# Two pairs' products with values in one TensorE step, short passes moved between VectorE and GpSimd, and unread products in TensorE's first planned waits

## The chip, the cores and the metric

The kernel runs on one core of one Trainium2 chip. Its time is device microseconds, the median over several executions. A profiled execution has a span (first to last recorded instruction) and a time of its own; both are given below. A core has five engines that run beside each other and wait on semaphores: TensorE (PE; its weight loads are PEld), VectorE (DVE), ScalarE (ACT), GpSimd (POOL), and SyncE (SP), which here issues all transfers, in order, from one queue.

## What is computed

Sliding-window attention with sink columns over 4 batches, 8 heads, 768 positions and a head size of 64, then a feed-forward layer over the 3072 x 512 result. The reference, cut:

```python
scores = scale * np.matmul(q, k.transpose(0, 1, 3, 2))
keep = (pos[None, :] < n_sink) | ((rel >= 0) & (rel < window))      # n_sink 4, window 128
a = softmax(np.where(keep, scores, -1e9))
x = heads_side_by_side(np.matmul(a, v))                             # 3072 x 512
h = np.maximum(x @ w_in, 0.0)                                       # 512 x 2048
out = (h * h) @ w_out                                               # 2048 x 512
```

## The kernel before

**Tiles.** The 3072 rows are eight chunks of 384 (half a batch each). In a chunk, heads go two by two: a *pair* has both heads on 128 partitions, and there are four pairs per chunk, 32 in all. Pairs 0 to 7 (the first two chunks) are *plain*: their scores are fp32 products on half the array each (L515). The other 24 have scores from operands split into a high and a low part, on the full array (L521).

**One pair's attention.** Per head and block of 128 queries: the scores go to one PSUM bank; VectorE scales, masks and takes the row maximum in one pass (L498); ScalarE takes the exponential and the row sum (L504). Then a small ScalarE pass (L593) and VectorE's reciprocal (L562) give the factor, and a scaling pass (L569 on GpSimd or VectorE, L567 on ScalarE) makes probabilities of it. The four sink columns go their own way. GpSimd copies them into a small buffer and subtracts the rounded part (`part_sinks`, L585 and L583, two short passes per head); for plain pairs TensorE transposes that buffer (L630), for the others VectorE does (L647) and four small transfers gather it (L653); a copy (L388) makes the operand `SK` of it. The window's probabilities are transposed too: for plain pairs on TensorE (L698, with copies out of PSUM by L388), for the others in 32 x 32 blocks on VectorE (L727, L731) into one array `T` for both heads, which four transfers put into DRAM (L744) and one gets back into `PT` (L757).

**Values.** `values` multiplies the transposed probabilities by the pair's values: for each head an fp32 product that takes half of the array's columns (L785; head 1 and head 0 beside each other), all into one PSUM bank, and then one full-array product for the sinks of both heads (L789, `VS` and `SK`). ScalarE copies the result as the high part of x (L801), VectorE subtracts it for the low part (L806).

**Feed-forward.** For each of 16 column blocks of the hidden layer (an *item*): twelve products with x (L837), a ReLU (L850) and a square (L854) on ScalarE, a product (L859) and a remainder (L866) on VectorE, then nine products with the second weights (L882). The weights come as packed 64-bit words; each of 32 rows costs VectorE four passes over 512 columns (L326, L333, L340, L350), the last of them sometimes on GpSimd, and ScalarE one (L346). The first chunks run as legs of 8, 16 and 8 items, the other six chunks as 16 items each.

**What sets the order.** All of this is handed to a `Plan`: `add(at, rank, emit, reads, writes, take, drop)` gives a step's engine or engines with a cost, a rank (its due time, counted in items), what it reads and writes, and the PSUM banks that it takes or frees. `order` then plays the engines forward by these costs and emits the steps in that order; on each engine the program runs in just that order. Banks: three for attention ("att"), two for the hidden layer, three for the output; the first chunk's attention may take any. A step marked "port" is one of VectorE's that GpSimd's steps keep clear of; with `SHARE` 0.5 an unmarked GpSimd step keeps clear of the first half of it. A switch of TensorE between full-array, half-row and half-column products is planned at 0.2.

## Time and profile before

| | us |
|---|---|
| median of three runs | 678.01 (lowest 676.47) |
| the profiled execution, its time | 677.97 |
| its span | 676.2 |
| TensorE busy / weight loads | 658.2 / 573.3 |
| VectorE busy | 445.5 |
| ScalarE busy | 392.5 |
| GpSimd busy | 125.2 |

In the profile, a row of the timeline has start, length, engine, line, operation, what it writes and reads, and how many instructions are merged; in brackets stand the idle time ahead of it and what ended that. In a list of stretches each engine has its busy time and its number of instructions, in the order PE, PEld, DVE, ACT, POOL, and then the granted TensorE clock, the share of the DMA engines and GB/s. A row of waits has the total, how often, and the longest. TensorE's matmuls are pipelined, and their ends are modelled: what one costs is best read from the start of one to the start of the next.

### The profile page before, as it was taken

To read this page: it belongs to the slowest core of one execution; us is meant where nothing else is said; L and a number is where in the kernel's file an instruction comes from. 1 tells how busy PE (TensorE), PEld (TensorE's weight loads), DVE (VectorE), ACT (ScalarE), POOL (GpSimd) and SP (SyncE) were. 2 spreads that over 40 slices of the span, in tenths; PEclk is the share of its full clock that TensorE was granted. 3 is DMA by queue.
4 is the path that set the end of the run, shared out by engine and by line. 5 is a ranking of instruction groups with operands and counts; after the bars stand their busy time and mean duration, and the time that the engine had idled before them with its cause. 6 is when DMAs were issued, how large, how long until landed. Compare 5 with 4: busy or idle time off the path is not lost.

```text
span 676.2 us, 11302 instructions
## 1 busy us (share of the span) xinstructions
PE 658.2 (97%) x3662; PEld 573.3 (85%) x3662; DVE 445.5 (66%) x1211; ACT 392.5 (58%) x1142; POOL 125.2 (19%) x319
## 2 busy tenths in 40 slices
PE   4999999999999999999999999999999999999996
PEld 3767889998888888898888888888889888899985
DVE  7899999878877656575667756665666664242221
ACT  5898644367665445566666676666677665542221
POOL 4542200033242221111112211111121221000000
PEclk9899999999999999999999999999999999999999
DMA  7856665025977544366555856557556853310001
GB/s 235 261 155 187 208 207 177 32 75 165 263 200 205 165 120 121 109 209 198 176 158 170 243 168 192 175 164 200 164 157 187 245 169 118 115 62 1 1 0 52
DMA packets 62547, 104.91 MB, mean 155 GB/s; under 512 B 10800, under 2 KB 39216, under 8 KB 62480
## 3 DMA queue, kind: packets, MB, share of 16 engines
q1 hardware_dynamic: 62480, 104.11, 51.8%
q8 instruction: 31, 0.51, 0.3%
q14 instruction: 36, 0.29, 0.1%
HBM read 78.72 MB, written 24.38 MB: 152 GB/s over the span
## 4 chain that ended last, share of the span: by engine, by line
PE 89%; DVE 7%; POOL 1%; issue 1%; DMA 1%; ACT 0%; SPq 0%; DVEq 0%; POOLq 0%
PE bank L882 39%; PE bank L837 38%; PE bank L785 5%; PE bank L521 5%; DVE P L498 2%; PE bank L789 1%; DVE w L350 1%; DVE f L333 1%; DVE f L340 1%; DVE f L326 1%; DVE P L569 1%; DMA kn<-in_k_dram 1%; POOL PSK_wide L585 1%; DVE gl L866 0%; PE bank L515 0%
## 5 line engine op out<-in xcount | busy, mean ns | idle before, releaser
L837 PE MATMUL bank<-x,w 128*128 128x384 f32 x1536 | 301.2, 338 | 0.0
L837 PEld LDWEIGHTS bank<-x,w 128*128 128x128 f32 x1536 | 266.1, 188 | 8.3 <-issue 1.4
L882 PE MATMUL bank<-w,gh 128*128 128x512 f32 x768 | 242.6, 397 | 0.0
L569 POOL TENSOR_SCALAR P<-P,small 128x260 f32<-128x260 f32 (+1 forms) x168 | 83.4, 513 | 415.6 <-DVE small L562 401.2
L882 PEld LDWEIGHTS bank<-w,gh 128*128 128x128 f32 x768 | 138.7, 188 | 22.4 <-issue 1.0
L882 PE MATMUL bank<-w,gl 128*128 128x512 f32 x384 | 151.8, 395 | 0.0
L850 ACT ACTIVATE r<-bank 128x384 f32<-128x384 f32 x128 | 62.7, 490 | 114.1 <-PE bank L837 112.8
L504 ACT ACTIVATE P<-P,nbs 128x260 f32<-128x260 f32 (+1 forms) x192 | 93.6, 488 | 60.3 <-DVE nbs L498 57.9
L859 DVE TENSOR_TENSOR bank<-bank,r 128x384 f32<-128x384 f32 x128 | 72.0, 563 | 77.4 <-ACT r L850 76.8
L498 DVE CUSTOM_DVE_ANT_0 P<-bank,maskA 128x260 f32<-128x260 f32 x128 | 53.1, 421 | 53.4 <-PE bank L521 52.8
L882 PEld LDWEIGHTS bank<-w,gl 128*128 128x128 f32 x384 | 72.1, 188 | 16.9
L866 DVE TENSOR_TENSOR gl<-bank,gh 128x384 fp32r<-128x384 f32 x128 | 71.1, 556 | 19.1 <-ACT gh L854 10.1
L854 ACT ACTIVATE gh<-r 128x384 fp32r<-128x384 f32 x128 | 66.7, 521 | 2.8 <-PE bank L882 0.7
L727 DVE STREAM_TRANSPOSE T<-P 128x384 f32<-128x384 f32 x96 | 45.3, 494 | 24.8 <-POOL P L569 24.7
L521 PEld LDWEIGHTS bank<-KS,QS 128*128 128x128 f32 x288 | 52.0, 188 | 5.7
L521 PE MATMUL bank<-KS,QS 128*128 128x260 f32 (+1 forms) x288 | 54.8, 277 | 0.0
L785 PE MATMUL bank<-PT,vn 128*64 128x256 f32 (+1 forms) x392 | 40.6, 347 | 0.0
L801 ACT CAST x<-bank 128x384 fp32r<-128x384 f32 x32 | 15.2, 474 | 42.1 <-PE bank L789 42.1
L785 PEld LDWEIGHTS bank<-PT,vn 128*64 128x64 f32 x392 | 25.7, 139 | 15.7 <-issue 6.3
L504 ACT ACTIVATION_READ_ACCUMULATOR P<-P,nbs 128x1 f32 x192 | 36.0, 188 | 0.0
L498 DVE CUSTOM_DVE_ANT_0 P<-bank,mask 128x128 f32<-128x128 f32 (+1 forms) x64 | 22.0, 353 | 19.3 <-PE bank L521 19.0
L374 ACT ACTIVATE sq<-sq,theta 128x256 bf16<-128x256 bf16 x64 | 32.2, 503 | 1.1
(99 smaller groups left out, 518.4 us busy)
## 6 DMA issues: line engine op xcount, KB each, us to landing
raw<-in_moe_w_dram SPq DMA_DIRECT2D x32, 512.0 KB, 4.0
half<-in_moe_w_dram SPq DMA_DIRECT2D x64, 256.0 KB, 3.9
via<-T SPq DMA_DIRECT2D x48, 192.0 KB, 3.1
PT<-via SPq DMA_DIRECT2D x12, 768.0 KB, 4.8
via<-T SPq DMA_DIRECT2D x48, 160.0 KB, 2.7
PT<-via SPq DMA_DIRECT2D x12, 640.0 KB, 5.4
kn<-in_k_dram SPq DMA_DIRECT2D x24, 264.0 KB, 3.9
qn<-in_q_dram SPq DMA_DIRECT2D x32, 192.0 KB, 3.7
```

Of the source, the lines that this page charges most:

```text
L498: nc.vector.tensor_tensor_reduce(Pt(h)[:, i, o : o + n], ps_[:, 0:n], mask[:, 0:n], -SCALE, BIG, ALU.add, ALU.min, nb)
L504: nc.scalar.activation(Pt(h)[:, i, o : o + n], Pt(h)[:, i, o : o + n], AF.Exp, bias=nb, scale=-1.0, accum_out=sm[:, h, i : i + 1],)
L521: nc.tensor.matmul(bank(key)[:, 0:n], QS(h)[:, cols], flat[:, a, c0 : c0 + n], start=(a == 0), stop=(a == 1),)
L569: {"POOL": nc.gpsimd, "DVE": nc.vector}[engine].tensor_scalar(a, a, rs[:, h, i : i + 1], 1.0, op0=ALU.mult, op1=ALU.mult)
L727: nc.vector.transpose(dst.rearrange("p c j b -> p j c b"), src.rearrange("p j (c b) -> p j c b", b=32))
L785: nc.tensor.matmul(xo[h * D : h * D + D, qs[0] * P : qs[0] * P + len(qs) * P], vn[:, kk, h, :], rhs(), start=(n == 0), stop=False, skip_gr ...
L837: nc.tensor.matmul(bank(key)[:, 0:TOK], wi[fc][:, i, cc * P : (cc + 1) * P], xt[:, cc, :], start=(cc == 0 and j == 0), stop=(cc == NCC - 1 ...
L850: lambda key=key, r=r: nc.scalar.activation(r(), bank(key)[:, 0:TOK], AF.Relu),
L854: ("ACT", 0.41), n - 9, lambda gh=gh, r=r: nc.scalar.activation(gh(), r(), AF.Square),
L859: lambda key=key, r=r: nc.vector.tensor_tensor(bank(key)[:, 0:TOK], bank(key)[:, 0:TOK], r(), op=ALU.mult),
L866: lambda key=key, gh=gh, gl=gl: nc.vector.tensor_tensor(gl(), bank(key)[:, 0:TOK], f32(gh()), op=ALU.subtract),
L882: nc.tensor.matmul(bank(okey), gt()[:, ts_], wo[f][:, i, :], start=(f == f0 and j == 0), stop=(f == f1 - 1 and j == 2),)
```

## The change

The edit has four parts and some that make room for them.

1. For pairs 8 to 31 the values of two pairs are one TensorE step: an even pair only leaves its functions in `waiting`; the odd pair's step runs both pairs' L785 products, into two banks, and then the first pair's sinks. The second pair's sinks are copied to `SK` after that and have a full-array step of their own. The step needs both pairs' transposed probabilities, so there are two arrays, `PT` and `PT2`, laid out by head. `T` holds one head instead of two; its four puts and the get are issued per head, the first head's with an earlier rank.
2. `part_sinks` may run on VectorE as well as on GpSimd, `SHARE` is 1.0 (an unmarked GpSimd step is planned behind the whole of a marked VectorE step), and the extra cost of a scaling pass on VectorE or ScalarE is 0.1 instead of 0.3.
3. Where the plan has TensorE wait more than 0.4 in the first 24 us for a step that takes a bank, `fill` writes products of the identity with itself into that bank; nothing reads them, and the step behind overwrites them.
4. The third chunk's attention has ranks that are six items earlier.

To make room: one array `G0` for the ReLU instead of two, one small `PSK` instead of two, the identity matrix lives in the scratch array `sq`.

```diff
-SHARE = 0.5
+SHARE = 1.0
-SC_DVE = 0.3
+SC_DVE = 0.1
+SOON = 6
+PS_DVE = 0.2
+WARM = 24.0
+FULL = 0.85
-SC_ACT = 0.3
+SC_ACT = 0.1
...
-        free = dict(PE=0.0, DVE=5.5, ACT=1.5, POOL=5.0, SP=0.5)
+        free = dict(PE=6.5, DVE=5.5, ACT=1.5, POOL=5.0, SP=0.5)
...
-                if chosen is None or a[0] < chosen[1][0] or (e == "POOL" and a[0] <= chosen[1][0] + 0.001):
+                if chosen is None or a[0] < chosen[1][0]:
...
             if e == "PE":
+                if picks and WARM > t > free[e] + 0.4:
+                    yield lambda i=picks[0], n=int((t - free[e] - 0.2) * FULL / 0.22): self.fill(i, n)
...
-                        ("POOL", 0.2), r - URGE + 0.01, lambda h=h: part_sinks(h, False),
+                        [("POOL", 0.2), ("DVE", 0.12, "port", PS_DVE)], r - URGE + 0.01, lambda e, h=h: part_sinks(e, h, False),
...
-                T = lambda: sb("T", [P, 4, 2 * NQ, 2, 32], F32, f"T_{s}")
+                T = lambda h: sb("T", [P, 4, 2 * NQ, 32], F32, f"T_{s}_{h}")
...
+                PTs = PT if s % 2 == 0 else sb("PT2", [P, 2, 4, 2 * NQ, 32], F32, "PT_1")
...
-                for x in range(4):
-                    add(
-                        ("SP", 0.42, 3.2, 180), rank(0.8), lambda x=x: put(x),
...
+                    for x in range(4):
+                        add(
+                            ("SP", 0.42, 2.9, 90), rank(0.8 if h else 1.2), lambda h=h, x=x: put(h, x),
...
+                for h in range(2):
+                    add(
+                        ("SP", 0.42, 3.5, 360), rank(0.5 if h else 0.9), lambda h=h: get(h),
...
+            elif p % 2 == 0:
+                waiting[0] = mine
+            else:
+                first, first_sinks, cells, first_key = waiting[0]
+                add(
+                    ("PE", 2 * spent + 0.2 + sunk, 2, 0), r, lambda: (first(), values(), first_sinks()),
+                    reads=[sk_cell, "VS"] + cells + mine[2], writes=[first_key, key_x],
+                    take=[("att", first_key), ("att", key_x)],
+                )
+                take_sinks()
+                add(("PE", sunk, 0), r, sink_values, reads=[sk_cell, "VS"], writes=[key_x])
+                parts(p - 1, first_key, *xs[slot[c]])
+                parts(p, key_x, *xs[slot[c]])
...
-                    r = lambda g=g: sb(f"G{g}", [P, TOK], F32, f"r_{g}")
+                    r = lambda: sb("G0", [P, TOK], F32, "r_0")
...
-                base, w = starts[nxt], (2.0 if nxt == 2 else 4.0)
+                base, w = starts[nxt] - (SOON if nxt == 2 else 0), (2.0 if nxt == 2 else 4.0)
...
+        def fill(i, n):
+            for _ in range(n):
+                nc.tensor.matmul(banks[i][:, 0:P], ident, ident, start=True, stop=True)
```

**How it moves instructions.** The lines of the changed kernel are numbered anew: values L798 (was L785), sinks' product L804 (L789), first products L872 (L837), second products L917 (L882), fills L1049, sinks' transposition L633 (L630), transpositions L705 (L698), the short passes L588 and L586 (L585 and L583), scaling L575 (L569).

TensorE, in the middle of the run, around one pair's values before:

```order
L837 MATMUL bank_70<-x_147,w_693 128x384
L785 MATMUL bank_67<-PT,vn_145 64x256 x4
L785 MATMUL bank_67<-PT,vn_145 64x128 x2
L789 MATMUL bank_67<-SK_128,VS 128x256
L837 MATMUL bank_70<-x_146,w_693 128x384 x2
L837 MATMUL bank_70<-x_147,w_693 128x384
L882 MATMUL bank_72<-w_668,gh_598 128x512 x2
```

and around two pairs' values in the change:

```order
L872 MATMUL bank_70<-x_145,w_725 128x384
L798 MATMUL bank_67<-PT,vn_142 64x256 x4
L798 MATMUL bank_67<-PT,vn_142 64x128 x2
L798 MATMUL bank_69<-PT_148,vn_143 64x256 x4
L798 MATMUL bank_69<-PT_148,vn_143 64x128 x2
L804 MATMUL bank_67<-SK_127,VS 128x256
L917 MATMUL bank_72<-w_720,gh_604 128x512 x2
L917 MATMUL bank_72<-w_720,gl_613 128x512
L917 MATMUL bank_73<-w_720,gh_604 128x512 x2
L917 MATMUL bank_73<-w_720,gl_613 128x512
L804 MATMUL bank_69<-SK_127,VS 128x256
```

Two visits to the half-column products have become one; the second pair's sinks' product stands between full-array products, some rows later.

TensorE at the start, from the last scores of the third pair to the first pair's values, in the change (`ident` alone is a fill; P_0_178 and P_1_184 are the first pair's two heads, P_205 the second pair):

```order
L521 MATMUL bank_68<-kn_164,qn_162 128x260
L1049 MATMUL bank_69<-ident 128x128 x9
L705 MATMUL bank_69<-ident,P_0_178 128x128 x4
L705 MATMUL bank_70<-ident,P_0_178 128x128
L705 MATMUL bank_70<-ident,P_1_184 128x128
L705 MATMUL bank_71<-ident,P_1_184 128x128 x4
L1049 MATMUL bank_72<-ident 128x128 x5
L633 MATMUL bank_72<-ident,PSK_wide 128x128 x2
L705 MATMUL bank_73<-ident,P_205 128x128 x4
L798 MATMUL bank_74<-PT,vn_142 64x128
```

Before there were no fills, and the second pair's four transpositions stood behind the values and not ahead of them; two more fills stand between the scores of the second and the third pair, one further behind.

GpSimd at the same place before (three scaling passes and both heads' short passes of the first pair):

```order
L569 TENSOR_SCALAR P_0_179<-P_0_179,small 128x128
L569 TENSOR_SCALAR P_0_179<-P_0_179,small 128x260
L569 TENSOR_SCALAR P_1_185<-P_1_185,small 128x260
L585 CAST PSK_wide<-P_0_179 128x2x2x4
L583 TENSOR_TENSOR PSK_wide<-P_0_179,PSK_wide 128x2x4
L585 CAST PSK_wide<-P_1_185 128x2x2x4
L583 TENSOR_TENSOR PSK_wide<-P_1_185,PSK_wide 128x2x4
L569 TENSOR_SCALAR P_206<-P_206,small 128x128
```

and in the change:

```order
L575 TENSOR_SCALAR P_0_178<-P_0_178,small 128x260
L575 TENSOR_SCALAR P_1_184<-P_1_184,small 128x260
L588 CAST PSK_wide<-P_1_184 128x2x2x4
L586 TENSOR_TENSOR PSK_wide<-P_1_184,PSK_wide 128x2x4
L575 TENSOR_SCALAR P_205<-P_205,small 128x128
```

One scaling pass and the first head's two short passes are gone from GpSimd; VectorE has the short passes behind its cast of the sinks' values, ahead of the first passes over the weights.

More of the change, by code (lines that the diff above doesn't have):

```diff
@@ L275, in sink_window_attention_moe @@
         PSKW = sb("w23", [P, 2, NQ, P], F32R, "PSK_wide")
[L276 removed]
+        for t in (VS, PSKW, PSK, *SK):
             nc.gpsimd.memset(f32(t), 0.0)
@@ L731, in turn, with put, get @@
                         nc.vector.transpose(dst, src.rearrange("p (c b) -> p c b", b=32))
+                via = lambda: dram(f"via{s % 2}", [2, 4, 32, 4, 2 * NQ, 32], f"via_{s}")
+                PTs = PT if s % 2 == 0 else sb("PT2", [P, 2, 4, 2 * NQ, 32], F32, "PT_1")
+                PT_cells = [("PT", x) for x in range(3)] if s % 2 == 0 else [("TP", x) for x in range(2)]
+                def put(h, r):
+                    nc.sync.dma_start(
+                        out=via()[h, :, :, r, 0:used].rearrange("c a i b -> a c (i b)"),
+                        in_=T(h)[32 * r : 32 * r + 32, :, 0:used].rearrange("a c i b -> a c (i b)"),
+                    )
+                def get(h):
+                    nc.sync.dma_start(
+                        out=PTs[:, h, :, 0:used].rearrange("p r i b -> p r (i b)"),
+                        in_=via()[h, :, :, :, 0:used].rearrange("c a r i b -> (c a) r (i b)"),
+                    )
                 for h in range(2):
-                    r = rank(1.3 if not plain and h == 0 else 0.9)
+                    r = rank(0.9 if h else 1.3)
                     for which in range(3 - i0):
@@ L799, in attention @@
-            xh, xl = xs[slot[c]]
-            add(
-                ("ACT", 0.4), r - URGE, lambda: nc.scalar.copy(xh[:, p, :], bank(key_x)[:, 0:TOK]),
-                reads=[key_x], writes=[("xh", slot[c], p)],
-            )
-            add(
-                ("DVE", 0.47), r - URGE,
-                lambda: nc.vector.tensor_tensor(xl[:, p, :], bank(key_x)[:, 0:TOK], f32(xh[:, p, :]), op=ALU.subtract),
-                reads=[key_x, ("xh", slot[c], p)], writes=[("xl", slot[c], p)], drop=[key_x],
-            )
+            spent, sunk = (1.07 if half == 0 else 1.28), (0.175 if i0 == 0 else 0.12)
@@ new lines, in parts @@
+            def parts(p, key_x, xh, xl):
+                add(
+                    ("ACT", 0.4), r - URGE, lambda: nc.scalar.copy(xh[:, p, :], bank(key_x)[:, 0:TOK]),
+                    reads=[key_x], writes=[("xh", slot[c], p)],
+                )
+                add(
+                    ("DVE", 0.47), r - URGE,
+                    lambda: nc.vector.tensor_tensor(xl[:, p, :], bank(key_x)[:, 0:TOK], f32(xh[:, p, :]), op=ALU.subtract),
+                    reads=[key_x, ("xh", slot[c], p)], writes=[("xl", slot[c], p)], drop=[key_x],
+                )
@@ L861, in products @@
                         ),
-                        reads=[("r", g)], writes=[(key, cc) for cc in range(NCC)],
+                        reads=["r"], writes=[(key, cc) for cc in range(NCC)],
                     )
```

100 lines of the change are left out of this document (47 added, 53 removed).

## The prediction

> **What bounds the kernel now.** I read the page's first two parts, then TensorE's waits, then busy time by stretch, and last the first 26 us engine by engine, because only there the page's slices are not full.
>
> ```profile
> span 676.2 us, 11302 instructions
> ...
> PE   4999999999999999999999999999999999999996
> ```
>
> TensorE is at 9 tenths or more in 38 of the 40 slices; only the first and the last are not. "Busy" is modelled, so the stretches have to confirm it:
>
> ```profile
> 80.00:100.00 20.00, 20.00 (x111) 17.75 (x110) 19.67 (x39) 9.04 (x17) 0.00 (x0) 1.00 0.63 202
> 200.00:300.00 100.00, 100.00 (x568) 87.92 (x565) 64.31 (x177) 51.33 (x142) 20.94 (x56) 1.00 0.53 153
> ```
>
> From 80 us on TensorE is busy without a gap. VectorE is 98% busy around there (19.67 of 20) and 64% later (64.31 of 100). So the end is set by two things: when TensorE's unbroken work begins, and how long that work is. A wait on another engine costs nothing unless it moves one of these two. The unbroken work is not all products, though. Here is one pair's products with values (L785, two halves of the array side by side; L789, the sinks' product, the full array) among the feed-forward's products, and a plain run of twelve L837:
>
> ```profile
> 304.25 1.73 PE L837 MATMUL bank<-x,w 128*128 128x384 f32 x9
> 305.92 1.30 PE L785 MATMUL bank<-PT,vn 128*64 128x256 f32 x12
> 307.15 0.38 PE L789 MATMUL bank<-SK,VS 128*128 128x256 f32 x1
> 307.37 0.69 PE L837 MATMUL bank<-x,w 128*128 128x384 f32 x3
> ```
>
> ```profile
> 334.79 2.12 PE bank L837 x12
> ```
>
> The last row is from the chain of work that ended last, whose pieces do not overlap; the others have a start and a length, and lengths overlap, so costs are read from start to start. Twelve L837 take 2.12 us, 0.177 each. The nine ahead of the visit take 1.67 us instead of 1.59: 0.08 lost on the way in. L789 with 256 columns takes 0.22 until the next L837 starts, where a 256-column product of that kind costs about 0.12 (0.177 x 256/384): 0.10 lost on the way out. Inside the visit, two looks at narrow windows:
>
> ```profile
> 306.18 0.82 PE L785 MATMUL bank<-PT,vn 128*64 128x256 f32 x6
> ```
>
> ```profile
> 306.62 0.60 PE L785 MATMUL bank<-PT,vn 128*64 128x256 f32 x6
> ```
>
> The second couple of products starts 0.26 us after the first (305.92 to 306.18), the next two 0.22 apart (306.18 to 306.62): 0.04 lost. From 306.62 there remain one couple at 0.21 and two half as long at 0.11, which end at 307.05; L789 starts at 307.15: 0.10 lost. Together 0.32 us per visit. The weight loader shows the same from its side, over all 24 visits of the later chunks:
>
> ```profile
> PEld bank L785 <- issue: 5.4, 21, 0.4
> PEld bank L789 <- issue: 4.1, 24, 0.2
> ```
>
> It idles 5.4/21 = 0.26 us ahead of L785 and 4.1/24 = 0.17 ahead of L789, 0.43 per visit, for no engine ("issue"). This bounds the price of a visit from above; the two ends that rows show outright (0.08 + 0.10) bound it from below at 0.18.
>
> **The first 26 us.** TensorE's first long wait, and what stands behind it:
>
> ```profile
> 10.36 1.33 PE L515 MATMUL bank<-kn,qn 64*128 64x128 f32 x10 [0.36 <-DMA kn<-in_k_dram]
> 12.87 0.93 PE L698 MATMUL bank<-ident,P 128*128 128x128 f32 x5 [1.17 <-POOL P L569]
> 13.96 0.77 PE L698 MATMUL bank<-ident,P 128*128 128x128 f32 x5 [0.16 <-POOL P L569]
> 17.83 0.69 PE L630 MATMUL bank<-ident,PSK_wide 128*128 128x128 f32 x2 [3.10 <-POOL PSK_wide L583]
> 18.45 2.40 PE L785 MATMUL bank<-PT,vn 128*64 128x128 f32 x12
> ...
> 21.16 2.06 PE L698 MATMUL bank<-ident,P 128*128 128x128 f32 x10
> ...
> 24.23 1.30 PE L785 MATMUL bank<-PTS,vn 128*64 128x128 f32 x12
> ...
> 42.81 0.52 PE L630 MATMUL bank<-ident,PSK_wide 128*128 128x128 f32 x3 [0.77 <-DVE nbs L498]
> ```
>
> ```profile
> 12.44 1.46 POOL L569 TENSOR_SCALAR P<-P,small 128x128 f32<-128x128 f32 x3 [5.41 <-DVE small L562]
> 13.85 0.38 POOL L585 CAST PSK_wide<-P 128x16 fp32r<-128x16 f32 x1
> 14.31 0.70 POOL L583 TENSOR_TENSOR PSK_wide<-P,PSK_wide 128x8 fp32r<-128x8 f32 x1
> 14.97 2.53 POOL L585 CAST PSK_wide<-P 128x16 fp32r<-128x16 f32 x1
> 17.57 0.20 POOL L583 TENSOR_TENSOR PSK_wide<-P,PSK_wide 128x8 fp32r<-128x8 f32 x1
> ```
>
> ```profile
> 13.56 0.62 DVE L401 CAST VS<-vs 24x512 fp32r<-24x512 f32 x1
> ...
> 15.56 1.27 DVE L333 SCALAR_TENSOR_TENSOR f<-raw,f 128x512 int32<-128x512 int32 x2
> 16.76 0.67 DVE L340 SCALAR_TENSOR_TENSOR f<-raw,f 128x512 int32<-128x512 int32 x1
> 19.21 0.19 DVE L562 RECIPROCAL small<-small 128x6 f32<-128x6 f32 x1 [1.77 <-ACT small L593]
> ```
>
> ```profile
> 14.29 1.31 ACT L388 COPY PT<-bank 128x512 f32<-128x512 f32 x3
> 18.61 0.36 ACT L388 CAST SK<-bank 32x256 fp32r<-32x256 f32 x1 [3.01 <-PE bank L630]
> ```
>
> ```profile
> 16.00:17.00 1.00, 0.00 (x0) 0.00 (x0) 1.00 (x3) 0.00 (x0) 1.00 (x1) 0.50 0.99 376
> ...
> 22.00:23.00 1.00, 1.00 (x8) 1.00 (x7) 0.95 (x3) 1.00 (x4) 0.89 (x5) 0.59 0.84 222
> ```
>
> GpSimd's second small cast (L585) took 2.53 us, the first 0.38. VectorE has L333 and L340 from 15.56 to 17.43, and the cast ends as they do (17.50). TensorE waits 3.10 us for it, ScalarE 3.01 for TensorE, VectorE 1.77 for ScalarE. During the wait the granted clock falls to 0.50 and comes back at about 22.8 us (0.59 in the mean of that slice): the first pair's values take 2.40 us where the second pair's take 1.30. After that TensorE's longest wait up to 62 us is the 0.77 at 42 us.
>
> **The change, part by part.** *Two pairs in one step.* The first eight pairs keep their own visits, the other 24 come two by two: 32 visits become 20. The first pair's sinks' product stays on the way out, the second's stands later between full-array products, where the rows give it no loss. 12 visits less at 0.35 us, a little above the 0.32 read from one visit because the loader's 0.43 is over all of them: **-4.2 us** (bounds 12 x 0.18 = 2.2 and 12 x 0.43 = 5.2). It all lies after 130 us, where TensorE never waits, so it should come off the end in full. In the order the plain scores' visits (L515) grow from 14 to 16; at the same price, and partly in waits: +0.3 (0 to 0.7).
>
> *The second transposed buffer, halved transfers.* The step needs both pairs' operands at once; PT2 holds the second. Transfers by head are 8 and 2 instead of 4 and 1 per pair, 120 more on SyncE's queue in all:
>
> ```profile
> via<-T SPq DMA_DIRECT2D x48, 192.0 KB, 3.1
> ...
> sk<-SKT SPq DMA_DIRECT2D x48, 12.0 KB, 2.2
> ```
>
> ```profile
> 311.04 1.55 SPq L744 DMA_DIRECT2D via<-T  x3
> ```
>
> A put of 192 KB lands after 3.1 us, one of 12 KB after 2.2, so half a put takes 2.2 to 3.1. One issue takes the queue about 0.5 us (three in 1.55), five more per pair 2.6 us of a pair's 19 to 20. The queue has that room, and the first head's transfers start earlier than before. Cost 0 on the path; what it costs without that cover is the slower rival.
>
> *VectorE takes one head's short passes, GpSimd's wait behind its long ones.* For the first pair GpSimd now has two scaling passes (1.46/3 = 0.49 each), one cast (0.38) and one subtraction (0.70, as at 14.31): 12.44 + 2.06 = 14.5, ahead of L333. VectorE's two short passes stand behind the cast of the sinks' values (13.56 + 0.62 = 14.18); no row has them on VectorE, so 0.15 to 0.47 each, by its smallest passes and by GpSimd's own mean; done at 14.5 to 15.1, taken 14.6. So the operand is ready at 14.6 instead of 17.77. But TensorE cannot take it then:
>
> *17 unread products.* Two, nine, five and one, ahead of four steps. One is a full fp32 product of 128 columns: between 0.15 us (a transposition of that shape: five in 0.77) and 0.31, since the trace records an fp32 product twice (L785 x12 for six in the order); I take 0.21, because the 0.77 holds the last one's full length. The last scores end at 11.69 (10.36 + 1.33), nine fills bring it to 13.6, ten transpositions to 14.9 (before 14.73, because five of them waited until 13.96), five fills to 15.9: the sinks' transposition comes 1.9 us earlier, not 3.2. Then ScalarE: its new order has two exponentials, a scaling pass and a small pass ahead of the copy that releases the values. From 14.3: copies 1.31, and by the nearest rows 0.3 to 0.5 for each of the four and 0.36 for the copy, 3.7 us in all: values at 18.0 instead of 18.45. At full clock they end at 19.3, with the sinks' product (0.22) 19.5 instead of 21.16: 1.7 us. The second pair's values, one clocked stretch later, some 1.9 (before 24.23).
>
> *What is left of it at 80 us.* VectorE loses its idle 1.77 us too, but its order puts more ahead: an estimate by each form's mean has 0.7 us more in front of the first multiplication (L859), and 0.6 to 2.4 more in front of the next seven. It is 98% busy there, so what it carries TensorE meets as waits. Between 1.9 kept and 0.5 lost, nearer the first because TensorE had other work through nearly all of that stretch (no wait over 0.77): **-1.5 us** (-3.5 to +0.5, the first if the earlier start also ends such waits).
>
> On the clock, the row comes first: it fell 1.3 us after the last transposition (14.73 to about 16.0), with TensorE busy for about half of the time since 10.36 (1.33 + 0.93 + 0.77 of 5.6 us), and stayed down for some 6.8. The Trainium skill, "TensorE: Matmul & The Clock Gate", Part 1, has the clock fall after an idle window of about 3.4 us, of windows that run freely. By that rule a wait of 3.10 us is too short to bring it down, and filling it gains nothing: the start loses the 1.1 us that 2.40 against 1.30 gave it. By the row the wait did bring it down; the trace here does not agree with the rule, and the sum goes by the row.
>
> *The rest.* One array for the ReLU instead of two, one small sink buffer instead of two, identity kept in a scratch array, the earlier attention of the third chunk: VectorE idles a third of its time after 130 us and TensorE shows no wait there, so 0; a miss would show as waits of L837 on VectorE.
>
> **The sum.** -4.2 + 0.3 - 1.5 = -5.4 us from this execution's 676.2 us span and 677.97 us time, which lies within 0.1 us of the median 678.01: 672.6 us, or 0.8% less.
>
> **The rivals.**
>
> *VectorE takes the start back.* It is as loaded as TensorE up to 100 us, and its order carries up to 2.4 us more. Against it: TensorE's longest wait there is 0.77 us. Then only the visits count: 677.97 - 4.2 + 0.3 = 674.1 us.
>
> *The fills do not hold the clock.* If the clock follows windows that fall elsewhere, the first values run at half speed whatever was filled: 18.0 + 2.40 + 0.3 = 20.7 against 21.16, a start worth 0.5: 677.97 - 4.2 + 0.3 - 0.5 = 673.6 us. Against it speaks that the 0.50 stretch follows that wait at once. The Trainium skill's rule above ("TensorE: Matmul & The Clock Gate", Part 1) speaks for it.
>
> *Slower: the single half-size T buffer.* VectorE cannot transpose the second head before the first head's four puts have read T: 4 x 0.5 + 2.7 = 4.7 us after. In its new order about 4.0 us of work lie between; at 64% busy that is 6.2 us, 1.5 to spare. If the puts stand behind a load that waits in SyncE's queue, VectorE stops with the hidden layer behind it. These rows of the page set what TensorE can bear:
>
> ```profile
> L859 DVE TENSOR_TENSOR bank<-bank,r 128x384 f32<-128x384 f32 x128 | 72.0, 563 | 77.4 <-ACT r L850 76.8
> ...
> L866 DVE TENSOR_TENSOR gl<-bank,gh 128x384 fp32r<-128x384 f32 x128 | 71.1, 556 | 19.1 <-ACT gh L854 10.1
> ...
> L850 ACT ACTIVATE r<-bank 128x384 f32<-128x384 f32 x128 | 62.7, 490 | 114.1 <-PE bank L837 112.8
> ```
>
> ReLU, product and remainder take 0.49 + 0.56 + 0.56 = 1.6 us, TensorE's next twelve products 2.1: 0.5 us of slack. Puts late by more than 1.5 + 0.5 = 2.0 us decide; at 2.5 each of 24 pairs loses 0.5: 677.97 - 5.4 + 12 = 684.6 us. Against it: TensorE shows no gap from 80 us on now (100.00 of 100).
>
> *The step comes late.* Both operands are awaited together and two of three attention banks are held; if each of 12 steps waits 0.35 us, the change does not do what it says: 676.8 us.
>
> **How the numbers follow.** Forecast 60% (672.6; its own range 670 to 675), VectorE takes it back 16% (674.1), no clock held 10% (673.6), late steps 4% (676.8), slower 6% (684.6), and 4% for a start that ends the small waits as well (3.5 instead of 1.5: 670.6 or less). The range 668 to 677.5 takes in all but the slower case and the edges. Two per cent, about what a measurement of this kernel can tell from no change, is 13.6 us: below 664.4 would need the whole visit bound (5.2) and over 8 us from a start whose waits are 3.10 and 1.2 (11.69 to 12.87) and whose half clock costs some 2.5: 2%. Above 691.6 would need the slower case doubled: 3%. Within: 95%.
>
> **What would show it.** After: loader idle ahead of the values' lines in about 12 places after 130 us and their sum near half of 9.5 us; no row like L585's 2.53 before 20 us; granted clock 1.00 from 10 us on; first values near 18 us, 1.3 us long; VectorE's 1.77 us wait gone; TensorE's last product some 5 us earlier. Wrong would be: waits of TensorE on VectorE or on PT after 130 us (then the slower rival), transpositions starting later than 14 us (fills too long), or an end moved by more than the visits with the same first 80 us.

## The result and the profile after

The changed kernel takes 671.23 us (671.18 to 671.27, four runs) where the kernel before took 678.21 beside it: a ratio of 0.990, 95% interval 0.989 to 0.992, so 6.6 us less, give or take 1. One execution of the kernel before took 1077.74 us; it counts in the 678.21, a median of four, and the ratio leaves it out. 672.6 was predicted. The profiled execution has this span and these slices of TensorE:

```profile
span 669.4 us, 11653 instructions
...
PE   7999999999999999999999999999999999999996
```

TensorE is full from the second slice on, as before. The start, which the prediction took apart, looks like this now (TensorE, then GpSimd, then VectorE; L1049 are the unread products, two records each):

```profile
10.37 1.19 PE L1049 MATMUL bank<-ident 128*128 128x128 f32 x4
11.49 1.37 PE L521 MATMUL bank<-kn,qn 64*128 64x128 f32 x12
12.79 2.27 PE L1049 MATMUL bank<-ident 128*128 128x128 f32 x18
14.91 1.25 PE L705 MATMUL bank<-ident,P 128*128 128x128 f32 x10
16.00 1.28 PE L1049 MATMUL bank<-ident 128*128 128x128 f32 x10
17.11 0.38 PE L633 MATMUL bank<-ident,PSK_wide 128*128 128x128 f32 x2
18.06 0.77 PE L705 MATMUL bank<-ident,P 128*128 128x128 f32 x4 [0.56 <-DVE P L575]
18.76 1.30 PE L798 MATMUL bank<-PT,vn 128*64 128x128 f32 x12
...
23.68 1.30 PE L798 MATMUL bank<-PTS,vn 128*64 128x128 f32 x12
```

```profile
15.20 0.24 POOL L588 CAST PSK_wide<-P 128x16 fp32r<-128x16 f32 x1 [0.29 <-DVE P L575]
```

```profile
12.02 0.29 DVE L504 CUSTOM_DVE_ANT_0 P<-bank,mask 128x128 f32<-128x128 f32 x1 [1.10 <-PE bank L521]
...
16.24 0.74 DVE L332 TENSOR_SCALAR f<-raw 128x512 int32<-128x512 int32 x2
16.91 0.67 DVE L339 SCALAR_TENSOR_TENSOR f<-raw,f 128x512 int32<-128x512 int32 x1
17.51 0.17 DVE L568 RECIPROCAL small<-small 128x6 f32<-128x6 f32 x1
17.72 0.67 DVE L575 TENSOR_SCALAR P<-P,small 128x128 f32<-128x128 f32 x2
```

GpSimd's cast of 2.53 us is gone: the one that stays there takes 0.24. The wait of 3.10 ahead of the sinks' transposition is gone too, the granted clock stays at 1.00 where it fell to 0.50 before (16 to 22.8 us), and the first pair's values take 1.30 us instead of 2.40. But they begin at 18.76, later than the 18.45 of before. Two rows tell why. The first two unread products and the steps behind them move the third pair's scores to 11.49 (10.36 before), and VectorE stands idle 1.10 us for them. And the second pair's transpositions, which now stand ahead of the first pair's values, start at 18.06, after a scaling pass of VectorE whose reciprocal (17.51) ran behind three passes over weights (16.24 to 17.5).

In the middle of the run, a step for two pairs among the feed-forward's products, and the weight loader's idle time from 140 us on, the stretch that the prediction used:

```profile
339.16 1.73 PE L872 MATMUL bank<-x,w 128*128 128x384 f32 x9
340.82 2.38 PE L798 MATMUL bank<-PT,vn 128*64 128x256 f32 x24
343.14 0.39 PE L804 MATMUL bank<-SK,VS 128*128 128x256 f32 x1
343.36 0.69 PE L872 MATMUL bank<-x,w 128*128 128x384 f32 x3
```

```profile
PEld bank L798 <- issue: 2.7, 10, 0.4
PEld bank L804 <- issue: 2.1, 12, 0.2
```

The two pairs' products take 2.32 us from start to start (340.82 to 343.14), where twice one pair's were 2.46; entry and exit are paid once. The loader idles 2.7 + 2.1 = 4.8 us there without an engine to blame, in 10 and 12 places; before it was 5.4 + 4.1 = 9.5, in 21 and 24. TensorE itself waits for nothing from 130 us to the end.

To see where time is won I use ScalarE's copies of finished output, since each kernel makes the same eight, at the ends of legs (a view of one line, its instructions grouped by engine):

```profile
L924 ACT COPY ob<-bank x8: 571/586/586, 92.9 to 668.8; 128x512 f32<-128x512 f32 x8
```

```profile
L959 ACT COPY ob<-bank x8: 579/586/590, 92.1 to 662.5; 128x512 f32<-128x512 f32 x8
```

The first copy comes 0.8 us earlier, the last 6.3 (6.36 by the rows' hundredths). So little of the gain lies at the start and most behind it. The first, the third and the last copy in every kernel of this study, in us:

| kernel | median | ratio to before, 95% interval | first copy | third copy | last copy |
|---|---|---|---|---|---|
| before | 678.2 to 678.6 | 1 | 92.89 | 289.78 | 668.83 |
| **changed** | 671.23 | 0.990, 0.989 to 0.992 | 92.06 | 285.65 | 662.47 |
| values one by one | 674.91 | 0.995, 0.993 to 0.996 | 92.05 | 288.69 | 666.89 |
| no unread products | 670.86 | 0.989, 0.988 to 0.991 | 91.44 | 285.04 | 661.86 |
| without the first two | 670.73 | 0.989, 0.987 to 0.991 | 91.09 | 284.68 | 661.50 |
| short passes on GpSimd | 673.83 | 0.993, 0.992 to 0.995 | 94.92 | 288.79 | 665.61 |
| before + short passes | 676.49 | 0.997, 0.996 to 0.998 | 91.10 | 287.76 | 666.82 |
| first part alone | 685.93 | 1.010, 1.008 to 1.011 | 92.90 | 300.60 | 677.42 |
| changed, third chunk not earlier | 683.62 | 1.008, 1.006 to 1.011 | 91.56 | 296.85 | 673.67 |
| room for the first part alone | 681.03 | 1.005, 1.003 to 1.006 | 91.35 | 294.10 | 672.29 |
| first and fourth part | 673.34 | 0.992, 0.990 to 0.993 | 93.35 | 287.53 | 664.35 |
| sinks apart | 672.08 | 0.991, 0.989 to 0.993 | 92.05 | 286.68 | 663.50 |
| plain pairs in twos, no unread | 670.59 | 0.989, 0.987 to 0.991 | 90.58 | 284.92 | 661.74 |
| plain pairs in twos, without the first two | 669.83 | 0.987, 0.986 to 0.989 | 90.03 | 284.33 | 661.15 |

Not all kernels ran on one chip; the kernel before ran beside each, so across rows the ratios are to be compared.

### The profile page after: what moved, and what is told of

Read it like the earlier page. It is cut to its first block, busy times and chain, and to the rows that moved or that the text cites. A ratio compares the mean times of both kernels' runs of the same rounds, so it can differ in the third digit from the quotient of the medians.

```text
span 669.4 us, 11653 instructions
## 1 busy us (share of the span) xinstructions
PE 656.5 (98%) x3696; PEld 576.2 (86%) x3696; DVE 441.5 (66%) x1210; ACT 393.6 (59%) x1156; POOL 118.6 (18%) x305
## 4 chain that ended last, share of the span: by engine, by line
PE 86%; DVE 11%; issue 1%; DMA 1%; ACT 0%; SPq 0%; DVEq 0%; POOL 0%
PE bank L917 37%; PE bank L872 37%; PE bank L798 5%; PE bank L527 5%; DVE f L339 2%; DVE w L356 1%; DVE f L346 1%; DVE P L504 1%; PE bank L521 1%; DVE f L332 1%; PE bank L804 1%; DVE P L575 1%; DVE gl L901 1%; DVE bank L894 1%; DMA kn<-in_k_dram 1%
## 5 line engine op out<-in xcount | busy, mean ns | idle before, releaser
L872 PE MATMUL bank<-x,w 128*128 128x384 f32 x1536 | 299.3, 338 | 0.0
L872 PEld LDWEIGHTS bank<-x,w 128*128 128x128 f32 x1536 | 265.5, 188 | 9.7 <-issue 2.4
L917 PE MATMUL bank<-w,gh 128*128 128x512 f32 x768 | 242.2, 396 | 0.6 <-DVE ob L959 0.6
L917 PEld LDWEIGHTS bank<-w,gh 128*128 128x128 f32 x768 | 138.3, 188 | 21.1 <-DVE ob L959 0.9
L575 POOL TENSOR_SCALAR P<-P,small 128x260 f32<-128x260 f32 (+1 forms) x159 | 81.0, 525 | 419.4 <-DVE small L568 414.1
L917 PE MATMUL bank<-w,gl 128*128 128x512 f32 x384 | 151.3, 394 | 0.0
L917 PEld LDWEIGHTS bank<-w,gl 128*128 128x128 f32 x384 | 72.0, 188 | 17.2
L798 PE MATMUL bank<-PT,vn 128*64 128x256 f32 (+1 forms) x392 | 36.9, 338 | 0.0
L798 PEld LDWEIGHTS bank<-PT,vn 128*64 128x64 f32 x392 | 25.3, 137 | 12.2 <-issue 3.1
L373 ACT ACTIVATE sq<-half 128x256 bf16<-128x256 f32 x64 | 27.2, 426 | 6.7 <-DMA half<-in_moe_w_dram 6.2
```

The costliest lines, as they stand in the source:

```text
L575: {"POOL": nc.gpsimd, "DVE": nc.vector}[engine].tensor_scalar(a, a, rs[:, h, i : i + 1], 1.0, op0=ALU.mult, op1=ALU.mult)
L798: nc.tensor.matmul(xo[h * D : h * D + D, qs[0] * P : qs[0] * P + len(qs) * P], vn[:, kk, h, :], rhs(), start=(n == 0), stop=False, skip_gr ...
L872: nc.tensor.matmul(bank(key)[:, 0:TOK], wi[fc][:, i, cc * P : (cc + 1) * P], xt[:, cc, :], start=(cc == 0 and j == 0), stop=(cc == NCC - 1 ...
L917: nc.tensor.matmul(bank(okey), gt()[:, ts_], wo[f][:, i, :], start=(f == f0 and j == 0), stop=(f == f1 - 1 and j == 2),)
```

## The experiments

**The visits.** Each pair's values in a step of their own again, the rest of the change kept:

```diff
-            elif p % 2 == 0:
-                waiting[0] = mine
             else:
...
+                if p % 2:
+                    take_sinks()
                 add(
-                    ("PE", 2 * spent + 0.2 + sunk, 2, 0), r, lambda: (first(), values(), first_sinks()),
...
+                    ("PE", spent + 0.2 + sunk, 2, 0), r, lambda: (values(), sink_values()),
```

> The changed kernel with each pair's values in a step of its own again (32 visits instead of 20); transfers by head, PT2, unread products and short passes stay. Theory 1, the visits are the gain: the switches of one visit cost 0.36 us (0.095 in, 0.05 and 0.10 inside, 0.10 and 0.106 out), so 12 more visits cost 4.4 us: 675.6 us; if the 1.4 us by which the other products stand closer after 130 us belong to the pairing too, 676.9. Rival, the gain lies in the start, the third chunk's earlier attention and the smaller transfers: less than 3 us lost, under 674 us.

Measured: 674.91 us; the first copy at the same time as in the changed kernel (92.05), the last 4.42 us later. Over twelve visits that is 0.368 each. (The five parts listed above add up to 0.45: the 0.10 inside, at the end, and the first 0.10 out are the same 0.10.) The start has no part in it, and TensorE's waits are the same in both kernels. So theory 1 holds in its first form: the visits are 4.4 us by the traces; ratios (0.9946 against 0.9902) and medians give 3.0 and 3.7, each uncertain by about 1.

**The unread products**, taken out:

```diff
-WARM = 24.0
+WARM = 0.0
```

> The changed kernel without the 17 unread products; the order of everything else stays. Theory 1, the unread products hold TensorE's clock: without them TensorE idles from about 12.8 us to the first transpositions at 14.9 and again ahead of the sinks' transposition, the granted clock falls below 0.6 between 16 and 20 us, the first pair's values take some 2.4 us instead of 1.30, and the time rises by about 1 us, to 672.2 us. Rival, the short passes on VectorE already keep the waits too short for the clock to fall: granted clock 1.00 throughout, first values within 0.3 us of 18.76 or earlier (the first two unread products, at half speed, pushed the third pair's scores back by 1.1 us), time 670.9 to 671.4 us.

Measured: 670.86 us, 0.6 us ahead of the changed kernel from the first copy to the last. Each theory is half right. The clock does fall (TensorE's rows, then the stretches, with the granted clock third from the end):

```profile
13.09 1.57 PE L705 MATMUL bank<-ident,P 128*128 128x128 f32 x10 [1.34 <-DVE P L575]
...
17.00 1.05 PE L705 MATMUL bank<-ident,P 128*128 128x128 f32 x4 [1.84 <-DVE P L575]
17.98 2.40 PE L798 MATMUL bank<-PT,vn 128*64 128x128 f32 x12
...
23.50 1.30 PE L798 MATMUL bank<-PTS,vn 128*64 128x128 f32 x12
```

```profile
17.00:18.00 1.00, 1.00 (x6) 0.58 (x6) 1.00 (x3) 1.00 (x5) 0.70 (x2) 0.67 1.03 243
18.00:19.00 1.00, 1.00 (x8) 0.81 (x9) 1.00 (x3) 1.00 (x4) 0.52 (x1) 0.50 1.09 251
20.00:21.00 1.00, 1.00 (x7) 0.69 (x5) 0.78 (x3) 0.17 (x2) 0.23 (x2) 0.62 0.90 219
```

0.67 in one slice and 0.62 in another put the half-speed stretch at 17.34 to 20.76, and the first values take 2.40 us. But they begin 0.78 us earlier, the second pair's begin 0.18 earlier in spite of the slow clock, and the lead stays. So the products hold the clock, and cost more than it is worth. The other traces say the same of the clock: in the seven kernels of the table that have unread products it does not fall at the start, in the seven without it falls between 16.0 and 18.3 us.

**Which of them cost.** Without the first two only:

```diff
+COLD = 10.5
...
-                if picks and WARM > t > free[e] + 0.4:
+                if picks and WARM > t > free[e] + 0.4 and free[e] > COLD:
```

> The changed kernel without the first two unread products only (those between the scores of the second and the third pair); nine, five and one stay. Theory 1, the first two cost the start 1.1 us, since they run at half speed ahead of the third pair's scores, and VectorE's chain carries the delay on: without them the third scores, the first scaling pass (12.7 instead of 13.8 us) and the first values (18.0 instead of 18.76) come as in the kernel without unread products, the clock stays at 1.00, and the time is 670.3 to 670.9 us. Rival, any unread product delays what stands behind it: the time stays at 671.2 us.

Measured: 670.73 us, and a lead of 0.97 us over the changed kernel in both copies: theory 1. By the medians it is 0.50. By the traces the other fifteen are worth 0.36 us (0.97 against 0.61), but one trace of each is not exact to that (see the start, below), and the medians, 670.73 and 670.86, cannot tell it either.

**The short passes**, back on GpSimd alone, with SHARE and the costs of scaling as before; the unread products stay:

```diff
-SHARE = 1.0
-SC_DVE = 0.1
-SC_ACT = 0.1
+SHARE = 0.5
+SC_DVE = 0.3
+SC_ACT = 0.3
...
-                        [("POOL", 0.2), ("DVE", 0.12, "port", PS_DVE)], r - URGE + 0.01, lambda e, h=h: part_sinks(e, h, False),
+                        [("POOL", 0.2), ("POOL", 0.2)], r - URGE + 0.01, lambda e, h=h: part_sinks(e, h, False),
...
-                if chosen is None or a[0] < chosen[1][0]:
+                if chosen is None or a[0] < chosen[1][0] or (e == "POOL" and a[0] <= chosen[1][0] + 0.001):
```

> The changed kernel with the short passes on GpSimd alone, SHARE 0.5 and the extra costs of scaling back at 0.3 (the second part undone); pairs in one step and unread products stay. Theory 1, VectorE's short passes give the start: GpSimd's second cast again takes over 2 us beside VectorE's long passes, the sinks' transposition comes near 17.5 us, the first values near 18.5 to 19, and the end is 0.3 to 0.9 us later: 671.5 to 672.1 us. Rival, only the clock mattered and the unread products hold it: first values within 0.3 us of 18.76 and 1.30 us long, time 671.0 to 671.4 us.

Measured: 673.83 us, a loss several times what I expected; the last copy 3.14 us later. The slow cast and the wait are back (GpSimd, TensorE, one of the stretches):

```profile
16.62 2.19 POOL L588 CAST PSK_wide<-P 128x16 fp32r<-128x16 f32 x1
```

```profile
19.15 0.44 PE L633 MATMUL bank<-ident,PSK_wide 128*128 128x128 f32 x2 [2.81 <-POOL PSK_wide L586]
```

```profile
18.00:19.00 1.00, 0.00 (x0) 0.00 (x0) 0.75 (x2) 0.00 (x0) 0.92 (x2) 1.00 1.05 224
```

The clock stays at 1.00 through a wait of 2.81 us. (In two of this kernel's five executions the mean clock is 0.994 and not 0.998, so it was not held in every one.) And yet the start is 2.0 us behind the kernel before (94.92 against 92.89), and 1.57 behind the kernel that has the first and the fourth part but no unread products (93.35, below; that one has the wait and the fall of the clock as well). Here, holding the clock without removing the wait is worth less than nothing.

The same part put alone into the kernel before:

```diff
-SHARE = 0.5
-SC_DVE = 0.3
-SC_ACT = 0.3
+SHARE = 1.0
+SC_DVE = 0.1
+SC_ACT = 0.1
...
-                        ("POOL", 0.2), r - URGE + 0.01, lambda h=h: part_sinks(h, False),
+                        [("POOL", 0.2), ("DVE", 0.12, "port", PS_DVE)], r - URGE + 0.01, lambda e, h=h: part_sinks(e, h, False),
```

> The kernel before with the second part alone: short passes on VectorE or GpSimd, SHARE 1.0, extra costs of scaling 0.1. Theory 1, it takes the 3 us wait ahead of the sinks' transposition away, first values near 18 us instead of 18.45, and about 1.4 us of it stay (kernels with and without it differ by that at 100 us): 677.1 us, between 675.9 and 677.6. Rival, VectorE sets the pace and takes it back: 678.2 to 678.8 us.

Measured: 676.49 us, 0.997 (0.996 to 0.998): 1.9 us less than the 678.40 beside it, and 2.01 us at the last copy. VectorE does not take it back. This is the largest single gain of the start, and the kernel before could have had it by itself.

**What the first part needs.** The pairs alone: short passes, SHARE, costs and the planner's tie rule as in the kernel with the short passes on GpSimd, and besides

```diff
-SOON = 6
-WARM = 24.0
-        free = dict(PE=6.5, DVE=5.5, ACT=1.5, POOL=5.0, SP=0.5)
+SOON = 0
+WARM = 0.0
+        free = dict(PE=0.0, DVE=5.5, ACT=1.5, POOL=5.0, SP=0.5)
```

> Only the first part of the change (two pairs' values in one step, with PT2 and transfers by head); short passes on GpSimd, no unread products, SHARE and costs as before, third chunk's attention not earlier. Theory 1, 12 visits fewer at 0.36 us, all of it off the end: 678.2 - 4.4 = 673.8 us, or 672.4 if the closer spacing of the other products comes with the pairing; the start is that of before (a wait of about 3 us ahead of the sinks' transposition, first values 2.4 us long). Rival, without the third chunk's earlier attention the paired steps come late: waits of TensorE after 100 us and a time above 675 us.

Measured: 685.93 us, 1.010 of before (1.008 to 1.011). The rival was right, and its bound of 675 lay 11 us too low: the first copy is where it was before, the third 10.8 us late. To see which of the parts left out is missed, the whole change without its earlier ranks for the third chunk:

```diff
-SOON = 6
+SOON = 0
```

> The changed kernel with the third chunk's attention at its old ranks (SOON 0); all else of the change stays. Theory 1, the paired step needs two pairs' operands and so the earlier ranks: TensorE waits for the values near 200 to 225 us as in the kernel with the first part alone, 12 to 15 us in all, time 683 to 686 us. Rival, the wait there came from GpSimd's short passes and the old costs: no such wait, 671 to 672.5 us.

Measured: 683.62 us, 12.4 us more than the changed kernel (11.2 at the last copy). It is the fourth part. TensorE's rows there, and the stretch around them:

```profile
206.08 2.40 PE L798 MATMUL bank<-PT,vn 128*64 128x256 f32 x12 [2.85 <-DVE nbs L504]
211.80 2.40 PE L798 MATMUL bank<-PT,vn 128*64 128x256 f32 x12 [3.31 <-DMA PT<-via]
```

```profile
205.00:210.00 5.00, 2.40 (x12) 1.25 (x12) 2.66 (x11) 2.40 (x8) 1.33 (x5) 0.50 0.88 219
210.00:215.00 5.00, 3.20 (x15) 2.09 (x15) 2.66 (x7) 0.25 (x1) 2.24 (x5) 0.50 0.54 180
```

Both pairs' operands are awaited: 2.85 us for the last scores' pass, then 3.31 for the transfer of the second pair. TensorE has nothing else by then, the clock goes to 0.50, and the products of both pairs of the step run at half speed (2.40 us for each pair). Is it the pairing or what made room for it? Only the room, each pair's values on their own (all else as in the kernel with the first part alone):

```diff
-                    ("PE", 2 * spent + 0.2 + sunk, 2, 0), r, lambda: (first(), values(), first_sinks()),
+                    ("PE", spent + 0.2 + sunk, 2, 0), r, lambda: (values(), sink_values()),
```

> Only what makes room for the first part: transfers by head, T for one head, PT2, one array for the ReLU, one small sink buffer, the identity in a scratch array; each pair's values stay a step of their own, short passes on GpSimd, no unread products, old ranks and costs. In the traces some 1.4 us of the gain lie neither at the start nor in the visits: other products stand closer from 140 us on. Theory 1, this comes with the new layout and the smaller transfers: 677.1 us. Rival, it belongs to the one profiled execution of the kernel before: 678.2 to 678.8 us. Third, the single buffers cost something without the rest: 679 us or more.

Measured: 681.03 us. The third outcome: the room costs by itself, at the same place. From the first copy to the last it takes 580.94 us, 5.0 more than before; the kernel with the first part alone, with twelve visits less, takes 8.6 more. TensorE's row there:

```profile
208.16 2.40 PE L798 MATMUL bank<-PT,vn 128*64 128x256 f32 x12 [2.23 <-DMA PT<-via]
```

So the room brings a pair's operands later, and a step for two pairs waits for the later pair as well. The row names the transfer back from DRAM, which points to the transfers by head through half a `T`; the pieces of the room were not tried one by one.

This run shows one thing more. Its short passes are all on GpSimd, in the order of the kernel before, but in the profiled execution none of them was slow (GpSimd and TensorE there, and two of VectorE's passes, before and there):

```profile
15.08 0.38 POOL L588 CAST PSK_wide<-P 128x16 fp32r<-128x16 f32 x1
```

```profile
16.45 2.12 PE L798 MATMUL bank<-PT,vn 128*64 128x128 f32 x12
```

```profile
14.88 0.75 DVE L326 TENSOR_SCALAR f<-raw 128x512 int32<-128x512 int32 x2
```

```profile
14.99 0.98 DVE L332 TENSOR_SCALAR f<-raw 128x512 int32<-128x512 int32 x2
```

The second cast took 0.38 us where it took 2.53 before, and VectorE's two passes beside it took 0.98 instead of 0.75. The values begin 2.0 us earlier than before, and the first copy comes at 91.35, near the 91.10 of the kernel before with the second part. So the slow pass is, by these traces, what the second part takes away, and the same order does not meet it in every execution.

The kernel with the first part alone, and the earlier ranks added:

```diff
-SOON = 0
+SOON = 6
```

> First and fourth part of the change (two pairs' values in one step, third chunk's attention six items earlier), without unread products and with the short passes and costs of before. Theory 1, the visits give 12 x 0.36 = 4.4 us once the earlier ranks take the wait at 200 us away: 674.1 us, or 672.7 if 1.4 us come with the layout. Rival, the step needs the second part too, so that a wait of several us stays: above 676 us.

Measured: 673.34 us, 0.992 (0.990 to 0.993). The wait at 200 us is gone, and from the first copy to the last this kernel is 4.94 us shorter than before (571.00 against 575.94).

**Where a switch's price sits.** The first pair's sinks in a step of their own too:

```diff
-                    ("PE", 2 * spent + 0.2 + sunk, 2, 0), r, lambda: (first(), values(), first_sinks()),
+                    ("PE", 2 * spent + 0.2, 2, 0), r, lambda: (first(), values()),
...
+                add(("PE", sunk, 0), r + 1, first_sinks, reads=[sk_cell, "VS"], writes=[first_key])
```

> The changed kernel with the first pair's sinks' product in a step of its own too, so that 11 of the 12 double steps end with a value product and are followed by another full-array product. Theory 1, the second loss on the way out (0.106 us behind the sinks' product) belongs to that product where it follows half-column products: 11 x 0.106 = 1.2 us less, 670.0 us. Theory 2, a switch costs the next two products 0.10 us each whatever they are: no change, 671.0 to 671.4 us.

Measured: 672.08 us, 0.8 us more. TensorE behind a double step:

```profile
303.33 2.38 PE L798 MATMUL bank<-PT,vn 128*64 128x256 f32 x24
305.65 0.74 PE L918 MATMUL bank<-w,gh 128*128 128x512 f32 x2
306.22 0.39 PE L918 MATMUL bank<-w,gl 128*128 128x512 f32 x1
306.45 0.63 PE L918 MATMUL bank<-w,gh 128*128 128x512 f32 x2
306.92 0.40 PE L918 MATMUL bank<-w,gl 128*128 128x512 f32 x1
```

The first two L918 behind the values take 0.57 us (305.65 to 306.22), the next two 0.47 (306.45 to 306.92): the 0.10 is paid by whichever product comes second. Theory 2 holds for the price: from the third copy to the last both kernels take 376.82 us. What is lost, 1.03 us in the traces, lies between the second and the third copy; 0.65 of it is a wait of TensorE near 174 us for VectorE's copy of finished output. Why that copy is later there, and where the rest goes, was not followed up.

**More visits less.** The second chunk's plain pairs two by two as well, without unread products:

```diff
+            if c == 1 and p % 2 == 0:
+                waiting[0] = (mine, sk_cell)
+            elif c == 1:
+                (first, first_sinks, cells, first_key), first_sk = waiting[0]
+                add(
+                    ("PE", 2 * spent + 0.2 + 2 * sunk, 2, 0), r, lambda: (first(), values(), first_sinks(), sink_values()),
...
-            if turned:
+            elif turned:
```

> The changed kernel without unread products, and with the values of the second chunk's four plain pairs two by two as well (18 visits instead of 20). Theory 1, a visit costs 0.36 us wherever it stands: 0.7 us less than without unread products, 670.1 us. Rival, before 100 us VectorE sets the pace and TensorE's saving is lost again in waits: 670.6 to 671.2 us; or the later values of the first pair of each couple hold up the second chunk, 672 us or more.

Measured: 670.59 us. At the first copy it leads the kernel without unread products by 0.86 us, at the last by 0.12: the lead is lost again before the third copy. The time is that of the rival's first form; its waits are not in the trace, where TensorE waits for nothing between 90 and 290 us, so what takes the lead back is not shown. And that together with all but the first two unread products:

```diff
+COLD = 10.5
...
-                if picks and WARM > t > free[e] + 0.4:
+                if picks and WARM > t > free[e] + 0.4 and free[e] > COLD:
```

> The changed kernel without the first two unread products, and with the values of the second chunk's four plain pairs two by two. Theory 1, the two add up: 0.97 us (the lead of the one kernel in the traces) and 0.1 (what the other gained over the kernel without unread products): 670.2 us. Rival, both end in VectorE's pace before 100 us: 670.6 to 671.2 us, no better than either.

Measured: 669.83 us (669.61 to 670.04), 0.987 (0.986 to 0.989), the fastest of this study; its last copy is 1.32 us ahead of the changed kernel's, where the two leads were to add up to 1.1. That is nearer to theory 1 (670.2) than to the rival.

## Why the prediction was right, and where it was not

**The bound** was read rightly: the time follows when TensorE's unbroken work begins and how long it is. The predicted gain of 5.4 us was 6.36 in the traces and 6.6 by the ratio. The terms came out like this:

| term | predicted | measured in the traces |
|---|---|---|
| visits to the value products | -4.2 | -4.42 (one by one against changed) |
| start | -1.5 | -0.83 (first copy) |
| plain visits | +0.3 | not seen apart |
| products closer everywhere | none | -1.0 to -1.3 (an estimate, below) |

**Visits.** Price and count held: the rows of one visit gave 0.32 us, the prediction took 0.35, and 0.368 was measured. The second pair's sinks' product, placed between full-array products, loses nothing, as assumed.

**Start.** The sum was mis-sized, and the step that failed is the one on the unread products. I counted nine and five of them at full speed and put the first two at nothing. These run at half speed, 0.43 us each, since the clock has not risen by 10.4 us; with the switches around them they put the third pair's scores back by 1.1 us, "the last scores end at 11.69" became 12.86, and the transpositions begin at 14.91, past the 14 us that the prediction named as the sign of fills too long. The kernel without the first two is 0.97 us ahead. VectorE has those scores' passes ahead of the first pair's reciprocal, so its whole chain moved. How much the two cost hangs on the moment at which the clock rises. The kernel whose third chunk is not earlier has the same order of TensorE here, and in its profiled execution the two took 0.67 us and not 1.12:

```profile
10.32 0.74 PE L1049 MATMUL bank<-ident 128*128 128x128 f32 x4
10.99 1.37 PE L521 MATMUL bank<-kn,qn 64*128 64x128 f32 x12
```

Its first values begin at 18.21 instead of 18.76, and its first copy comes 0.5 us earlier. So a start that is read from one trace is uncertain by about half a microsecond, 0.83, 0.97 and 0.61 among them. The estimate for the values, 18.0 us, is near what the kernels without unread products (17.98) and without the first two (17.86) show. The mechanism behind that number was another, though: I let ScalarE's copies release the values, while TensorE's own order did, by the second pair's transpositions ahead of them.

The short passes were worth more than the -1.5 for the whole start (1.8 us alone at the first copy, 2.0 at the last), and the rival "VectorE takes the start back" fell with that run: 92.89 to 91.10 at the first copy, and nothing of it lost by the last.

**The clock.** That unread products hold it was right. My reading of what makes it fall was not: I set a wait of 3.10 us beside a length of 3.4. A wait of 1.84 us brought the clock down in the kernel without unread products, one of 2.81 did not in the kernel with the short passes on GpSimd. The length of one wait does not decide. In the run before, the stretch ahead was

```profile
15.00:16.00 1.00, 0.00 (x0) 0.00 (x0) 1.00 (x3) 0.60 (x2) 1.00 (x2) 0.99 1.06 418
```

which puts the fall at 15.98, and the 0.59 at 22 us puts the return at 22.82: 6.84 us at half speed, twice the 3.42 of the kernel without unread products (17.34 to 20.76). Half-speed stretches come in multiples of one length: near 200 us, in the kernel whose third chunk is not earlier, it is 10.24 us, three times (0.98 in the slice from 204 and 0.90 in that from 215 put it at 204.96 to 215.20). The Trainium skill, "TensorE: Matmul & The Clock Gate", Part 1, has windows of about 3.4 us that run freely, and the traces agree with the length and with the free run. That a window must be idle they do not bear out as it stands: in the 3.4 us ahead of the fall at 15.98 (from 12.57) TensorE was busy for 1.70 us, with ten transpositions and no other product. What a window must hold to keep the clock up is not shown. So the rival that named this rule was wrong in its conclusion, that a wait of 3.10 us is too short; in the length and the free run the rule itself holds.

**"The rest: 0"** was wrong in a way that the total hides. The earlier attention of the third chunk is not free decoration: without it the change is 0.8% slower than before. The prediction's slower rival (half a `T`, late puts and gets) names the mechanism, priced it at 12 us, spread over 24 pairs, and argued against it with TensorE's full slices. Those slices were of a kernel without the longer chain. The price came out, 12.4 us, but by another way, so that is luck: VectorE does wait for the puts near there (1.21 and 1.28 us), yet what costs is one stretch, 200 to 222 us, in which TensorE waits for its values' operands and runs at half clock, and not 0.5 us in each of 24 pairs. The half puts were no dearer than said, 2.0 us to land:

```profile
via<-T SPq DMA_DIRECT2D x96, 96.0 KB, 2.0
```

**What no term foresaw.** The last leg has no attention in it, and takes 65.14 us before (first fence) and 65.02 in the changed kernel:

```profile
603.69 0.59 ACT L924 COPY ob<-bank 128x512 f32<-128x512 f32 x1 [0.33 <-PE bank L882]
...
668.83 0.59 ACT L924 COPY ob<-bank 128x512 f32<-128x512 f32 x1 [2.43 <-PE bank L882]
```

```profile
597.45 0.59 ACT L959 COPY ob<-bank 128x512 f32<-128x512 f32 x1 [0.34 <-PE bank L917]
...
662.47 0.59 ACT L959 COPY ob<-bank 128x512 f32<-128x512 f32 x1 [2.39 <-PE bank L917]
```

It is 65.14 in the kernel before with the short passes too, and 65.02 in the kernel that has only the room. So 0.18% comes with the room for the first part (the one array for the ReLU, `T` by head, `PT2`, the small buffer, the identity's place). From the third copy to the last, past its wait, the kernel with the room alone takes 378.19 us against 379.05 before, 0.23%. Over the 576 us from the first copy on that is an estimate of 1.0 to 1.3 us, and it closes the sum (0.83 + 4.42 + 1.0 to 1.3 = 6.3 to 6.6, measured 6.36). Which of these buffers does it was not tried and stays open.

## What to carry to other kernels

Where an engine is never idle, what it loses between its own instructions can be read from start to start around one odd step; that price times a count holds within a few per cent. An edit that joins two steps makes them wait for the later of two operands: look for what brings that one earlier, and price the join without it. Before filling a wait with useless work, see whose chain stands behind the filled engine: hold the clock where nothing is queued behind, and remove the wait if it can be removed. A pass that is slow in one execution and not in another of the same order cannot be priced from one trace.

## What the runs showed of the hardware

- In the executions read above the clock fell and returned 3.42 us apart, or 6.84, or 10.24: once, twice and three times one length. The first rise to full speed comes at another moment in each execution: at 9.2 us in the run before (the scores' spacing goes from 0.42 to 0.21 us), after 11.1 in the changed kernel (unread products still 0.213 us a record then, 0.112 at 13 us).
- Going to half-column products and back costs the next two products each time: about 0.09 and 0.05 us on the way in, 0.10 and 0.10 on the way out, whatever the second product is.
- GpSimd's cast of 16 columns takes 0.24 to 0.52 us, or 2.19 to 2.53 when VectorE's 512-column passes over weights hold it up; it then ends 0.06 to 0.07 us behind the last of these (17.50 against 17.43 in the run before). In the execution of the kernel with the room alone the same cast got through in 0.38 us, and VectorE's passes took 0.23 us longer. Which of the two engines waits differed between executions with the same order of passes.
